# Where float64 weights are converted and where the softmax is divided: one change to a fused attention and Fourier-mixing kernel

## The chip, the cores and the metric

The kernel runs on 1 core of one Trainium2 chip. The metric is the device time in microseconds (us) of one launch; the median of seven runs is given. The engines of the core are TensorE (PE in the profile, its weight loads PEld), VectorE (DVE), ScalarE (ACT), GpSimd (POOL) and SyncE (SP), which here issues nearly all transfers. TensorE writes to PSUM; the other engines take its results from there.

## The reference

Eight batches of eight heads, 576 rows, head size 64. Attention keeps only the scores within `tau` of the row's maximum. Its result, with the heads joined to 512 columns, is transformed by a Fourier transform over rows and columns (the real part is kept), added to itself, normalized and sent through two matrix products with a ReLU between.

```python
scores = (1 / sqrt(64)) * q @ k.T                       # per batch and head
thresh = max(scores, axis=-1) - tau
scores = where(scores >= thresh, scores, -1e9)
attn = exp(scores - max(scores)); attn /= sum(attn) + 1e-9
x = (attn @ v) joined to (8, 576, 512)
mixed = real(fft(fft(x, axis=1), axis=2))
u = x + mixed
un = (u - mean(u)) / sqrt(var(u) + 1e-6)
out = u + maximum(un @ w_ch1, 0) @ w_ch2                # w_ch1 (512, 2048), w_ch2 (2048, 512)
```

`w_ch1` and `w_ch2` come as float64. [...]

## The kernel before

**Pairs and steps.** Two heads make a pair, four pairs a batch, so there are 32 pairs. A pair has five steps: four of 128 rows of q and one of the last 64. That makes 160 steps, 20 in each batch; step `i` belongs to pair `i // 5`. A step runs

- `scores` (L410): PE multiplies q and k into two PSUM tiles `sc`, of which there are two, so the next scores wait until DVE has read the last ones;
- `softmax` (L437): DVE finds the maxima (L448), ACT takes the exponential (L456) and the threshold (L460), DVE cuts off and sums (L464), adds 1e-9 and takes the reciprocal `den` (L476);
- `transposed_weights` (L493) of the step before: PE transposes `e` into `pe` (L516) and `pw` (L533), ACT copies them out to `ends` (L523, L528) and `e_t` (L535, L537);
- for the last step of a pair `weighted_values` (L542): PE multiplies with `v` into `pv` (L554), and the result goes to `x`. For half of the pairs two rows of `x` are then swapped by four small transfers.

`prep_pair` (L379) transposes q and k of the next pair (`pq`, `pk`, `pt`), and DVE and ACT copy them to `qT` and `kT`.

**Where the softmax is divided.** In the first two batches POOL spreads `den` over a tile `rec` (L486), PE transposes `rec` too (L519) beside `e` into `pe`, both parts go to `ends`, and DVE multiplies `pv` with it (L562). From the third batch on (`normalized`, L405) DVE multiplies `e` by `den` at once (L480), there is no `rec`, and ACT copies `pv` to `x` (L560).

**Mixing and channels.** When a batch's `x` is there, it is folded (`fold_rows`, `fold_halves`: POOL, for the last pair DVE) and goes through `mixing` (L624: PE `py`, `pa`; the sums into `u_t` by DVE and POOL). Then `channels` (L717) takes groups of 384 rows: `ph` with `w1` (L744), ReLU into the four sections `h0` to `h3` (L750 on ACT, L752 on DVE), then `po` with `w2` (L765) and the result out. Both are generators, which `fill` (L789) advances three times in each step from the second batch on, by a budget of PE work, so that PE's order mixes attention and channels. PSUM holds four tiles `mm` for all of this. In the first batch `busy` (L102) puts products of a constant (L109, `pd`) into the order as filler, two units in steps before `NCHUNK` and one after, each unit two matmul records.

**Conversion.** A chunk is 512 KB of float64. `convert` (L273) is a generator of five parts: the transfer (L280); two bit operations on DVE (L290, L293); three activations on ACT (L298, L301, L304); one product and sum on DVE (L306); two products on POOL (L311, L312). `w1` has 16 chunks, `w2` has 16. A chunk needs room for its raw bits and for the powers. In the first batch the room is a section of `h` (`staged`), and steps 0 to 19 convert `w1` and the last four chunks of `w2` (`first_chunk`, `NCHUNK` = 20), one started in each step. In the second batch `PLAN` (L887) lists the other 12: the step, the chunk, its room (a pair of chunks of `w2` not yet written, a section of `h`, or the tile `tmp`) and the step that issues its transfer. The powers then go to the part of `u_t` that the second batch does not use yet. `advance` runs the next part of a step's chunk. In the second batch the order is by hand on all engines (`second_batch`, L930); from the third on it is by hand on PE alone, and a scheduler places the others.

```python
w2_chunk(j):  pairs_w2 holds chunks (0,1), (2,3), (4,5); chunks 6 to 15 have tiles of their own
room 0, 1, 2: the raw bits lie in pairs_w2[room], that is, in both chunks of that pair
```

Of the kernel before, what the change touches and what calls it, by code (L numbers as in the profile page):

```python
# [47 lines left out]
def kernel(  # L48
# [270 lines left out]
    def staged(n, src, dst):  # L319
        stage = sb.tile([128, 3, WC], INT32, tag=f"h{n % 4}", bufs=1, name="stage")  # L320
        return chunk(src, dst, stage[:, 0:2, :], stage[:, 2, :])

    def first_chunk(n):

        if n >= HID // WC * ND:
            return staged(n, *w2_chunk(NJ - 1 - (n - HID // WC * ND)))
        g, c = divmod(n, ND)
        cols = slice(WC * g, WC * (g + 1))
        return staged(n, w_ch1[128 * c : 128 * (c + 1), cols], w1[c][:, cols])
# [4 lines left out]
    def second_chunk(j, room):  # L334


        if room == "h":
            return staged(3, *w2_chunk(j))
        if room == "tmp":
            raw = sb.tile([128, 2 * WC], INT32, tag="tmp", bufs=1, name="stage")[:, :]  # L340
        else:
            raw = pairs_w2[room][:, :].bitcast(INT32)
        power = u_t[:, j % ND, S : S + WC].bitcast(INT32)
        return chunk(*w2_chunk(j), raw.rearrange("p (c n) -> p c n", c=2), power)
# [34 lines left out]
    def prep_pair(n):  # L379
# [22 lines left out]
        if n + 1 < B * NPAIR:  # L402
            load_pair(n + 1)

    def normalized(n):  # L405


        return n >= 2 * NPAIR

# [27 lines left out]
    def softmax(i, between=None, meanwhile=None):  # L437
# [38 lines left out]
        nc.vector.reciprocal(den[:, 0:nh], den[:, 0:nh])  # L476
        rec = None
        if normalized(i // NT):
            for j in range(nh):
                nc.vector.tensor_scalar(  # L480
                    out=e[:, S * j : S * (j + 1)], in0=e[:, S * j : S * (j + 1)],
                    scalar1=den[:, j : j + 1], scalar2=None, op0=ALU.mult,
                )
        else:
            rec = sb.tile([128, 2 * D], FP32, tag="rec", name="rec")
            nc.gpsimd.tensor_copy(  # L486
                rec[:, :].rearrange("p (j d) -> p j d", j=nh), _repeated(den[:, 0:nh], 2 * D // nh)
            )
        if t == 4:
# [3 lines left out]
    def transposed_weights(i):  # L493
# [22 lines left out]
        nc.tensor.transpose(pe[:, 0, :], e[:, 512:640], ident[:, :])  # L516
        parts = 1
        if rec is not None:
            nc.tensor.transpose(pe[:, 1, :], rec[:, :], ident[:, :])  # L519
            parts = 2  # L520
        if t < 4:
            qs = slice(128 * t, 128 * t + 128)
            nc.scalar.copy(ends[:, 0:parts, qs], pe[:, 0:parts, :])  # L523
        else:
            qs = slice(512, S)
            for j in range(2):
                hp = slice(64 * j, 64 * j + 64)
                nc.scalar.copy(ends[hp, 0:parts, qs], pe[hp, 0:parts, hp])  # L528
        for j in range(2 if t < 4 else 1):
# [12 lines left out]
    def weighted_values(n):  # L542
# [6 lines left out]
        for h in range(2):  # L549
            cols = slice(HALF * h, HALF * (h + 1))  # L550
            pv = ps.tile([128, 512], FP32, tag="mm", bufs=4, name="pv")
            for c in range(5):
                for j in range(2):
# [4 lines left out]
                    )  # L558
            if normalized(n):
                nc.scalar.copy(x[:, cols], pv[:, 0:HALF])  # L560
            else:
                nc.vector.tensor_tensor(  # L562
                    out=x[:, cols], in0=pv[:, 0:HALF], in1=ends[:, 1, cols], op=ALU.mult
                )
        if p % 2:
# [151 lines left out]
    def channels(g):  # L717
# [4 lines left out]
        rstd = sb.tile([128, nt], FP32, tag="rstd", name="rstd")  # L722
        hT = [sb.tile([128, 4, GT], FP32, tag=f"h{i}", bufs=1, name=f"h{i}") for i in range(4)]

# [15 lines left out]

        for j in range(NJ):
            ph = ps.tile([128, 512], FP32, tag="mm", bufs=4, name="ph")
            for c in range(ND):
# [61 lines left out]
    def step(i):  # L805
# [28 lines left out]
        if i > 0 and i + 3 < NCHUNK:  # L834
            chunks[i + 3] = first_chunk(i + 3)
        if t == 2 and n > 0:
# [6 lines left out]
    after = []  # L843
    NCHUNK = HID // WC * ND + 4

# [19 lines left out]

    chunks = {0: first_chunk(0)}
    raw = load_dim()
    load_seq()
    chunks[1] = first_chunk(1)
    prep_pair(0)  # L870
    load_v(0)
    chunks[2] = first_chunk(2)
    chunks[3] = first_chunk(3)
    load_v(1)
# [9 lines left out]
    while after:  # L884
        after.pop(0)[1]()

    PLAN = (  # L887
        (2, 11, 0, 0), (3, 10, 1, 0), (4, 9, 2, 0), (5, 8, 0, 3), (6, 7, 1, 4), (7, 6, 2, 5),
        (8, 5, 0, 6), (9, 4, 1, 7), (10, 3, "h", 7), (11, 2, 0, 9), (12, 1, "tmp", 9),
        (14, 0, "tmp", 13),  # L890
    )
    chunks = {-1: chunks.pop(NCHUNK - 1)}

    def advance(at):
        if at in chunks:
            next(chunks[at], None)

    def transfers(first):
        for at, j, room, issue in PLAN:
            if issue == first:  # L900
                chunks[at] = second_chunk(j, room)

# [27 lines left out]
    def second_batch(i):  # L930
# [6 lines left out]
        softmax(i, None, lambda: advance(first - 1))  # L937
        if first - 1 in chunks:
            next(chunks.pop(first - 1), None)
        transfers(first)  # L940
# [13 lines left out]
        elif first == 1:  # L954
            mix(3)
            transposed_weights(i - 1)
            busy(2)
            mix(2)
        elif first == 2:
            mix(2)  # L960
# [9 lines left out]
        else:  # L970
            fill()
            transposed_weights(i - 1)
            advance(first)
            advance(first)
            if t == 3:
                prep_pair(n + 1)
            fill()
            fill()
# [85 lines left out]
```

## Time and profile before

| what | us |
|---|---|
| median of 7 runs | 1754.01 (1752.21 to 1757.78) |
| time of the profiled execution | 1754.01 |
| its span, first to last instruction | 1752.0 |
| first batch (reciprocal of step 0 to that of step 20) | 15.4 to 142.8 |
| second batch (to the reciprocal of step 40) | 142.8 to 302.7 |
| last attention step's reciprocal (step 159) | 1526.6 |

Some groups of the page, with the mean time of one and the count:

| line, engine | what | mean ns | count |
|---|---|---|---|
| L744 PE | `ph`, 384 columns | 490 | 1536 |
| L765 PE | `po`, 512 columns | 597 | 1152 |
| L533 PE | transposes of `e` | 274 | 1152 |
| L519 PE | transposes of `rec` | 277 | 40 |
| L480 DVE | `e` times `den` | 572 | 216 |
| L486 POOL | `rec` | 369 | 40 |
| L560 ACT | `pv` to `x` | 399 | 48 |
| L562 DVE | `pv` times `rec` to `x` | 450 | 16 |

Matmuls are pipelined: the mean is the duration of one, and the distance between two starts is shorter. The granted clock over the whole span is 0.997. The page's chain of waits lies on PE for 82% of the span, on DVE for 7% and on ACT for 4%.

### The profile page before, as it was taken

What the parts mean: (1) busy time and instruction counts of PE and PEld (TensorE: products, weight loads), DVE (VectorE), ACT (ScalarE), POOL (GpSimd) and SP (SyncE); (2) the same over time, 40 slices, a digit from 0 to 9 for tenths busy, and PEclk for the clock granted to TensorE, in tenths of its full rate; (3) what the DMA queues carried; (4) which work ended last, traced back from release to release, by engine and by line L of the source; (5) the groups of instructions that cost most, each with busy time, mean ns of one, the idle gap of its engine ahead of it and who ended that gap; (6) DMA issues with size and microseconds to landing.
All of it is one profiled execution on the core that took longest, in us unless ns stands there. A gap on an engine that the chain in (4) does not pass through costs nothing.

```text
span 1752.0 us, 21426 instructions
## 1 busy us (share of the span) xinstructions
PE 1708.3 (98%) x7772; PEld 978.9 (56%) x7772; DVE 858.4 (49%) x2123; ACT 662.4 (38%) x1510; POOL 317.3 (18%) x499
## 2 busy tenths in 40 slices
PE   8988989999999999999999999999999999999999
PEld 4555655555565566566555556556556556555453
DVE  6786765544445555544433655644334555511010
ACT  5674664323243444334233435333224334411010
POOL 5575542030110311020110212011101031010000
PEclk9999999999999999999999999999999999999999
DMA  5331311100100101010010110100001010000000
GB/s 158 107 100 57 101 55 36 33 14 14 32 21 20 27 22 33 21 33 14 17 30 14 27 33 22 27 26 24 10 26 27 24 29 9 1 12 7 12 7 18
DMA packets 130350, 57.00 MB, mean 33 GB/s; under 512 B 121123, under 2 KB 121125, under 8 KB 130246
## 3 DMA queue, kind: packets, MB, share of 16 engines
q1 hardware_dynamic: 128854, 55.35, 11.8%
q8 instruction: 62, 1.02, 0.2%
q10 hardware_dynamic: 1392, 0.30, 0.1%
q14 instruction: 42, 0.34, 0.1%
HBM read 46.02 MB, written 9.44 MB: 32 GB/s over the span
## 4 chain that ended last, share of the span: by engine, by line
PE 82%; DVE 7%; ACT 4%; issue 3%; POOL 1%; DMA 1%; SPq 1%; ACTq 0%; DVEq 0%; POOLq 0%
PE ph L744 27%; PE po L765 27%; PE pv L554 8%; PE sc L420 7%; PE pw L533 5%; DVE e L464 2%; PE sc L431 2%; ACT e L456 1%; PE py L653 1%; DVE neg L448 1%; PE pa L670 1%; PE pa L674 1%; PE pe L516 1%; PE pn L728 1%; PE pk L394 1%
## 5 line engine op out<-in xcount | busy, mean ns | idle before, releaser
L744 PE MATMUL ph<-u_t,w 128*128 128x384 f32 x1536 | 522.9, 490 | 4.0 <-ACT ends L523 1.2
L765 PE MATMUL po<-w,h 128*128 128x512 f32 x1152 | 524.3, 597 | 0.0
L744 PEld LDWEIGHTS ph<-u_t,w 128*128 128x128 f32 x1536 | 282.7, 190 | 191.7 <-issue 13.9
L448 DVE TENSOR_REDUCE neg<-sc 128x1 f32<-128x576 f32 x288 | 205.7, 751 | 357.3 <-PE sc L420 281.0
L456 ACT ACTIVATE e<-sc,neg 128x576 f32<-128x576 f32 x288 | 211.9, 736 | 352.8 <-DVE neg L448 351.8
L765 PEld LDWEIGHTS po<-w,h 128*128 128x128 f32 x1152 | 207.9, 190 | 221.4 <-issue 220.2
L464 DVE SCALAR_TENSOR_TENSOR e<-sc,thr,e 128x576 f32<-128x576 f32 x288 | 227.4, 814 | 86.2 <-ACT thr L460 82.9
L420 PE MATMUL sc<-kT,qT 64*128 64x288 f32 x1024 | 166.8, 431 | 4.5 <-DVE e L464 3.8
L533 PE MATMUL pw<-ident,e 128*128 128x128 f32 x1152 | 155.0, 274 | 11.9 <-ACT kT L395 5.8
L533 PEld LDWEIGHTS pw<-ident,e 128*128 128x128 f32 x1152 | 130.9, 141 | 39.5 <-issue 14.4
L750 ACT ACTIVATE h<-ph 128x384 f32<-128x384 f32 x96 | 47.1, 491 | 263.5 <-PE ph L744 263.4
L535 ACT COPY e_t<-pw 128x512 f32<-128x512 f32 x256 | 140.0, 593 | 11.0 <-PE pw L533 10.3
L420 PEld LDWEIGHTS sc<-kT,qT 64*128 64x128 f32 x1024 | 92.9, 187 | 83.6 <-issue 58.0
L585 POOL TENSOR_TENSOR half<-x 128x287 f32<-128x287 f32 x48 | 40.3, 860 | 542.2 <-ACT x L560 238.8
L692 POOL TENSOR_TENSOR u_t<-x,tmp 128x289 f32<-128x289 f32 (+1 forms) x47 | 36.3, 782 | 539.7 <-DVE tmp L689 539.3
L752 DVE TENSOR_SCALAR h<-ph 128x384 f32<-128x384 f32 x96 | 53.1, 554 | 162.0 <-PE ph L744 161.9
L480 DVE TENSOR_SCALAR e<-e,den 128x576 f32<-128x576 f32 x216 | 115.4, 572 | 3.4
L772 DVE SCALAR_TENSOR_TENSOR u<-po,rstd,u 128x512 f32<-128x512 f32 x36 | 26.9, 747 | 123.1 <-PE po L765 123.1
L560 ACT COPY x<-pv 128x288 f32<-128x288 f32 x48 | 19.2, 399 | 149.9 <-PE pv L554 133.8
L554 PE MATMUL pv<-e_t,v_rev 128*64 128x288 f32 x512 | 68.3, 409 | 0.6 <-ACT h L750 0.6
L554 PE MATMUL pv<-e_t,v_in 128*64 128x288 f32 x512 | 68.4, 409 | 0.0
L523 ACT COPY ends<-pe 128x128 f32<-128x128 f32 (+1 forms) x128 | 37.2, 291 | 71.7 <-PE pe L516 62.9
(147 smaller groups left out, 1499.8 us busy)
## 6 DMA issues: line engine op xcount, KB each, us to landing
stage<-in_moe_w_ch_dram SPq DMA_DIRECT2D x23, 512.0 KB, 4.0
out_dram<-u SPq DMA_DIRECT2D x36, 256.0 KB, 2.0
qk_in<-in_q_dram SPq DMA_DIRECT2D x64, 128.0 KB, 2.4
v_in<-in_v_dram SPq DMA_DIRECT2D x64, 128.0 KB, 2.3
w<-in_moe_w_ch_dram SPq DMA_DIRECT2D x9, 512.0 KB, 3.7
qk_in<-in_k_dram SPq DMA_DIRECT2D x31, 128.0 KB, 2.4
qk_in<-in_k_dram SPq DMA_DIRECT2D x31, 64.0 KB, 2.3
qk_in<-in_k_dram SPq DMA_DIRECT2D x93, 16.0 KB, 2.1
```

Source lines behind the costliest of these rows:

```text
L420: nc.tensor.matmul(sc[j][:, c, 0:HALF], qT[hp, 128 * t : 128 * t + 128], kT[hp, HALF * c : HALF * (c + 1)], start=True, stop=True,)
L448: nc.vector.tensor_reduce(out=neg[:, j : j + 1], in_=sc[j][:, :, 0:HALF], axis=AXIS_XY, op=ALU.max, negate=True,)
L456: nc.scalar.activation(out=ej, in_=sc[j][:, :, 0:HALF], func=ACT.Exp, bias=neg[:, j : j + 1], scale=1.0)
L464: nc.vector.scalar_tensor_tensor(out=ej, in0=sc[j][:, :, 0:HALF], scalar=thr[:, j : j + 1], in1=ej, op0=ALU.is_ge, op1=ALU.mult, accum_out ...
L480: nc.vector.tensor_scalar(out=e[:, S * j : S * (j + 1)], in0=e[:, S * j : S * (j + 1)], scalar1=den[:, j : j + 1], scalar2=None, op0=ALU.mult,
L533: nc.tensor.transpose(pw[:, c, :], e[:, c0 : c0 + 128], ident[:, :])
L535: nc.scalar.copy(e_t[:, 4 * j : 4 * j + 4, qs], pw[:, :, :])
L554: nc.tensor.matmul(pv[64 * j : 64 * j + 64, 0:HALF], vt[:, 2 * c + j, :], e_t[:, 4 * j + c, cols] if c < 4 else ends[:, 0, cols], start=(c ...
L744: nc.tensor.matmul(ph[:, 0:GT], w1[c][:, 128 * j : 128 * (j + 1)], u_t[:, c, c0 : c0 + GT], start=(c == 0), stop=(c == ND - 1),)
L750: nc.scalar.activation(out=ht, in_=ph[:, 0:GT], func=ACT.Relu)
L752: nc.vector.tensor_relu(ht, ph[:, 0:GT])
L765: nc.tensor.matmul(po[:, :], hT[j // 4][:, j % 4, 128 * t : 128 * (t + 1)], w2[j], start=(j == 0), stop=(j == NJ - 1),)
```

## The change

It has four parts.

1. `normalized` goes. In all 160 steps POOL makes `rec`, PE transposes it, `ends` gets two parts, and DVE multiplies `pv` with it.
2. The first batch converts only `w1` (16 chunks, `w1_chunk`). As `NCHUNK` falls to 16, steps 16 to 19 have one unit of filler where they had two (three units in all, since step 16 has none).
3. `PLAN` has all 16 chunks of `w2`. The first four lie in `h0` to `h3`; steps 5, 8 and 9 convert two chunks each; a step holds a list of chunks, and step 1 advances too. `channels` allocates a section of `h` when it comes to it and not all four at once.
4. In the second batch `prep_pair` comes after the second `fill` of its step and not before. In PE's order this moves q and k in step 38 alone: two `po` products come ahead of `pq`.

```diff
-        rec = None
-        if normalized(i // NT):
-            for j in range(nh):
-                nc.vector.tensor_scalar(
-                    out=e[:, S * j : S * (j + 1)], in0=e[:, S * j : S * (j + 1)],
-                    scalar1=den[:, j : j + 1], scalar2=None, op0=ALU.mult,
-                )
-        else:
-            rec = sb.tile([128, 2 * D], FP32, tag="rec", name="rec")
-            nc.gpsimd.tensor_copy(
-                rec[:, :].rearrange("p (j d) -> p j d", j=nh), _repeated(den[:, 0:nh], 2 * D // nh)
-            )
+        rec = sb.tile([128, 2 * D], FP32, tag="rec", name="rec")
+        nc.gpsimd.tensor_copy(
+            rec[:, :].rearrange("p (j d) -> p j d", j=nh), _repeated(den[:, 0:nh], 2 * D // nh)
+        )
...
-        parts = 1
-        if rec is not None:
-            nc.tensor.transpose(pe[:, 1, :], rec[:, :], ident[:, :])
-            parts = 2
+        nc.tensor.transpose(pe[:, 1, :], rec[:, :], ident[:, :])
...
-            if normalized(n):
-                nc.scalar.copy(x[:, cols], pv[:, 0:HALF])
-            else:
-                nc.vector.tensor_tensor(
-                    out=x[:, cols], in0=pv[:, 0:HALF], in1=ends[:, 1, cols], op=ALU.mult
-                )
+            nc.vector.tensor_tensor(
+                out=x[:, cols], in0=pv[:, 0:HALF], in1=ends[:, 1, cols], op=ALU.mult
+            )
...
-        hT = [sb.tile([128, 4, GT], FP32, tag=f"h{i}", bufs=1, name=f"h{i}") for i in range(4)]
+        hT = []
...
         for j in range(NJ):
+            if j % 4 == 0:
+                i = j // 4
+                hT.append(sb.tile([128, 4, GT], FP32, tag=f"h{i}", bufs=1, name=f"h{i}"))
...
-    NCHUNK = HID // WC * ND + 4
+    NCHUNK = HID // WC * ND
...
     PLAN = (
-        (2, 11, 0, 0), (3, 10, 1, 0), (4, 9, 2, 0), (5, 8, 0, 3), (6, 7, 1, 4), (7, 6, 2, 5),
-        (8, 5, 0, 6), (9, 4, 1, 7), (10, 3, "h", 7), (11, 2, 0, 9), (12, 1, "tmp", 9),
-        (14, 0, "tmp", 13),
+        (1, 15, "h0", 0), (2, 14, "h1", 0), (3, 13, "h2", 0), (4, 12, "h3", 0),
+        (5, 11, "0", 0), (5, 10, "1", 0), (6, 9, "2", 0), (7, 8, "h3", 5),
+        (8, 7, "0", 6), (8, 6, "1", 6), (9, 5, "tmp", 4), (9, 4, "h3", 8),
+        (10, 3, "0", 9), (11, 2, "h3", 10), (12, 0, "tmp", 10), (14, 1, "tmp", 13),
     )
-    chunks = {-1: chunks.pop(NCHUNK - 1)}
+    chunks = {}
...
     def advance(at):
-        if at in chunks:
-            next(chunks[at], None)
+        for run in chunks.get(at, ()):
+            next(run, None)
...
         elif first == 1:
             mix(3)
             transposed_weights(i - 1)
             busy(2)
             mix(2)
+            advance(first)
+            advance(first)
...
             advance(first)
             advance(first)
+            fill()
             if t == 3:
                 prep_pair(n + 1)
             fill()
-            fill()
```

## The prediction

> **What bounds the kernel now.** I read the page's busy shares first, then a table of windows by stage, then the timeline where the stages meet.
>
> ```profile
> PE 1708.3 (98%) x7772; PEld 978.9 (56%) x7772; DVE 858.4 (49%) x2123; ACT 662.4 (38%) x1510; POOL 317.3 (18%) x499
> ```
>
> PE is busy for 98% of the span, but that average hides stages. In the windows below the columns are: length, then the busy time of PE, PEld, DVE, ACT and POOL, the granted clock, the DMA share and GB/s. 115:143 is the end of the first batch, 142:310 the second batch, the other four the third to eighth batch (steps 40 to 159).
>
> ```profile
> 115.00:143.00 28.00, 22.91 (x135) 13.52 (x133) 25.07 (x60) 21.02 (x43) 20.99 (x24) 1.00 0.35 100
> 142.00:310.00 168.00, 156.34 (x844) 94.61 (x841) 110.04 (x268) 90.07 (x197) 68.34 (x90) 0.99 0.21 59
> ...
> 310.00:541.90 231.90, 230.11 (x997) 131.28 (x996) 104.93 (x260) 79.87 (x185) 25.05 (x42) 1.00 0.09 22
> 541.90:953.50 411.60, 409.08 (x1905) 236.12 (x1904) 205.42 (x517) 153.04 (x357) 49.03 (x84) 1.00 0.10 24
> 953.50:1365.00 411.50, 408.98 (x1905) 236.12 (x1904) 206.26 (x517) 153.13 (x357) 49.19 (x84) 1.00 0.10 24
> 1365.00:1530.00 165.00, 162.85 (x824) 95.84 (x823) 94.49 (x242) 69.52 (x163) 23.86 (x40) 1.00 0.07 17
> ```
>
> From 310 to 1530 PE lacks only 1220.0 - 1211.0 = 9.0 us, while DVE is busy for half of the time: there an instruction more on PE lengthens the run, and one less on DVE does nothing. From 115 to 143 it is the other way round: DVE 25.1 of 28 us, and PE's 22.9 contain filler (L109). In the second batch PE lacks 11.7 us, so only what makes PE wait counts.
>
> **Third to eighth batch: 120 transposes come back.** In each of the 120 steps from step 40 on, `rec` is transposed on PE once more, as L519 does in the first 40 steps. Its price is the distance between starts, not its duration:
>
> ```profile
> 122.27 0.27 PE L516 MATMUL pe<-ident,e 128*128 128x128 f32 x1
> ...
> 122.37 0.27 PE L519 MATMUL pe<-ident,rec 128*128 128x128 f32 x1
> ...
> 122.48 1.04 PE L533 MATMUL pw<-ident,e 128*128 128x128 f32 x8
> ...
> 542.15 0.27 PE L516 MATMUL pe<-ident,e 128*128 128x128 f32 x1
> ...
> 542.26 0.60 PE L533 MATMUL pw<-ident,e 128*128 128x128 f32 x4
> ```
>
> The columns are start and duration in us. With `rec` the first `pw` starts 0.21 us after `pe`, without it 0.11; the eight of one group take 1.04, so (1.04 - 0.27) / 7 = 0.11 each. 120 x 0.109 = **+13.1 us**. Lower bound: PE's idle 9.0 us all hide it, 4.1. Upper bound: none overlaps its neighbours, 120 x 0.272 = 32.6. I take 13.1, as the trace shows that very sequence at that distance in the first 40 steps and the groups of eight at it everywhere.
>
> The Trainium skill ("TensorE: Matmul & The Clock Gate", Part 4: PE-mode transpose) gives about 275 ns for a transpose in a kernel's context; priced so, the 120 would be 33 us and the whole forecast near 1781.6. That figure agrees with the duration of one in this trace (272), but the distance of starts decides, so the measurement is followed.
>
> Beside it, at no cost:
> - 216 multiplications of `e` leave DVE (L480, 115.4 us). Nothing waits on DVE there; the gain is between 0 and the 9.0 us, and PE's few idle places in that stretch are mostly released by ACT (`ends`, `kT`) or POOL: 0.
> - 120 copies of `rec` come to POOL (L486, median 316 ns, 38 us) beside 147 of 1220 us busy. The transpose waits for the copy, and all of PE's order stands behind it, but it comes one step later (8 to 10 us), so the copy has a step's time. In the 40 existing ones PE and PEld waited 3.3 us in all; at that rate 120 would cost 10 us. Most of those stood behind conversions on POOL, which the later batches lack: 0, upper end 10.
> - The product of L562 (450 ns x48 on DVE) replaces ACT's copy L560 (399 ns x48). `ends` is held until it ends; the next writer of `ends` comes after scores (1.24) and a unit of `ph` (2.85), over 4 us of cover. Without the cover 48 x 0.45 = 21.6.
> - `ends` is copied 256 wide instead of 128 (0.37 against 0.28 us): 96 x 0.09 = 8.6 us of ACT, hidden by four PSUM buffers.
>
> **End of the first batch: four conversions leave.** Chunks 16 to 19 were w2's. Each costs DVE 0.487 + 0.596 + 0.778 = 1.86, ACT 2.0 and POOL 2.6 us. What it costs the chain is how long a finished score waits for its reduction behind them:
>
> ```profile
> 128.94 1.20 PE L431 MATMUL sc<-kT,qT 64*64 64x288 f32 x10 [0.17 <-DVE e L464]
> ...
> 130.12 0.79 DVE L290 TENSOR_SCALAR w<-stage 128x512 int32<-128x512 int32 x1
> ...
> 130.82 1.01 DVE L293 TENSOR_SCALAR stage<-stage 128x512 int32<-128x512 int32 x1
> ...
> 131.75 1.28 DVE L306 SCALAR_TENSOR_TENSOR w<-stage,w 128x512 f32<-128x512 uint32 x1
> ...
> 132.96 0.74 DVE L448 TENSOR_REDUCE neg<-sc 128x1 f32<-128x576 f32 x1
> ```
>
> Here the scores end at 130.14, the reduction starts at 132.96: 2.8 us. In the two steps before the same gap is 0.4 (120.51 to 120.89) and 0.45 (125.77 to 126.22), in the step after it nothing. Sum **-3.7 us**; ends 0 and -7.4 (all four conversions' DVE time). The second batch starts that much earlier, and PE's chain follows.
>
> Three filler pairs (L109, 0.86 us per unit of two matmuls) go in steps 17 to 19; they run while PE waits, so 0. If the granted clock fell for it, the price is what the one dip shows at 255.83: eight `ph` in 3.79 instead of 2.85, 0.9 us. The skill speaks against taking filler away (same page, "Why this matters for your kernels": no idle gaps over about 3 us); at the rate of the dip it would add 0.9 us. PE's longest gap in that window is 2.83 us, and the clock read 1.00.
>
> **Second batch: sixteen conversions for twelve.** Where they delay PE:
> - Chunk 15 is new in steps 21 and 22. Its DVE pair (1.08) comes after 161.77, its three ACT operations (2.0) before the exponential that started at 162.47: that then starts near 164.3, and `sin` (L685, 164.38), for which PE's `pw` waits already, 1.8 later. **+1.8**; ends 0 and 3.1.
> - Two chunks in steps 25, 28, 29. The second adds DVE 0.498 + 0.821, ACT 2.0, in the next step DVE 0.8. Step 25 has the 4.8 us of `pv` as cover; in step 26 the second L306 stands before the product that frees the scores (PE came at 201.71, it ended at 201.59): +0.8. In step 28 it fills a DVE wait of 2.24 us on POOL: 0. In step 29 ACT's 2.0 stand before the exponential (225.74) and the ReLU (227.17) for which `pv` waited: +1.7. **+2.5**; ends 0 and 10 (three times 1.3 + 2.0).
> - Other rooms for the chunks take waits away, and q and k go one unit later in step 38:
>
> ```profile
> 250.32 0.69 DVE L290 TENSOR_SCALAR w<-stage 128x512 int32<-128x512 int32 x1 [3.04 <-POOL w L312]
> ...
> 252.16 0.66 PE L389 MATMUL pq<-ident,qk_in 128*128 128x128 f32 x4 [2.56 <-DVE h L752]
> ...
> 254.71 1.12 PE L394 MATMUL pk<-ident,qk_in 128*128 128x128 f32 x4 [1.90 <-ACT ends L523]
> ...
> 288.93 0.66 PE L389 MATMUL pq<-ident,qk_in 128*128 128x128 f32 x4 [1.48 <-ACT ends L523]
> ```
>
> Brackets hold the idle time before and its releaser. Chunk 1 overwrites half of the tile in which chunk 2 is still staged, so DVE waits for POOL, a ReLU is late, PE stands for 2.56 + 1.90, and the dip adds 0.9: 5.4. A like wait of 3.06 at 231.87 ends in a PE gap of 1.2 at 239.02. In the new order chunks 4 and 5, 2 and 3, 0 and 1 come a step or more after the last reader of their pair. With the 1.5 at 288.93 (two `po` products, 1.7 us, now run there) 8.1 us can go. But three transfers (chunks 4, 3, 2) now have one step between the POOL product that frees their room and their use: 2.9 to 5.6 us of POOL and 4.0 to land, against steps of 6.5 to 11.6, so some wait comes back. **-6.0**; ends -8.1 and 0.
> - SP: seven transfers of 512 KB instead of three stand before `load_v` in the first step. At the page's 158 GB/s they take 23 us; that `v` is used five steps (45 us) on: 0. In step 30 the swap of `x` rows stands behind a transfer that waits for POOL, about when the swap was issued before (236.4): 0.
> - Sections of `h` allocated as reached: an order of buffers only, 0; the last chunk in `h3` ends two steps before its section.
>
> **Sum** against the profiled execution (1754.01 us, span 1752.0 and 2.0 around it; its time is the median of the seven): 13.1 - 3.7 + 1.8 + 2.5 - 6.0 = **+7.7, 1761.7 us**. The last 222 us (`ph` and `po` alone) are untouched.
>
> **Rivals.**
> - *Faster.* The first two batches give back more than the transposes take. At hand are PE's idle 5.1 and 11.7 us and 2.6 of filler, 19.4; to be faster by 3.5 it takes 16.6, 86% of it: 1750.5 at that point. For it: DVE is the bound at 115 to 143. Against: of the 11.7 only 7.1 stand at the four gaps named above; the rest, at the folds, the mixing and the first `ph`, keeps what makes it. Chance 0.06.
> - *Nothing measurable.* As forecast, but waits and conversions at their good ends, half of chunk 15 and the pairs hidden: 13.1 - 5.5 + 1 + 1 - 8.1 = +1.5, 1755.5. Chance 0.14.
> - *Late `rec`.* POOL takes its order strictly; where a fold of `x` (about 4 us, waiting for the swap's DMA) stands before the copy, PE's transpose waits. At 1 us in each of 12 pairs with a swap +12: 1773.7. Against: in the built order the copy stands before those folds. Chance 0.08.
> - *Crowded second batch.* The doubled steps cost 10 instead of 2.5 and the waits come back: 13.1 - 3.7 + 1.8 + 10 = +21, 1775. Chance 0.08.
>
> The forecast itself keeps 0.64, with its own range of 1757.5 to 1767.
>
> **Range.** 1755 to 1769 leaves out the faster case, a part of the second and most of the last two. What a measurement can tell from no change is 0.2%, 3.5 us: faster 0.06, same 0.14, slower 0.80.
>
> **What would show it.** From the third batch on each pair of batches 411.5 + 40 x 0.109 = 415.9 long, with 160 `rec` transposes in all and PE's idle no larger; step 20's reciprocal near 139 instead of 142.8; the gap before `pq` at 252 gone. It is wrong if PE shows waits on POOL's `rec` after 310, or if the second batch ends more than 8 us earlier or any later than before.

## The result and the profile after

The changed kernel takes 1759.46 us (median, 1758.03 to 1760.61); the kernel before, measured beside it, 1753.78. The ratio is 1.0028, with a 95% interval of 1.0021 to 1.0035: slower by about 4.9 us (the medians are 5.7 apart). Between the two profiled executions the span grows by 6.0 us, from 1752.0 to 1758.0; the trace below explains these 6.0.

First the busy shares and the windows of the changed kernel, in the columns and the stretches used before:

```profile
PE 1716.3 (98%) x7886; PEld 989.9 (56%) x7886; DVE 776.6 (44%) x1955; ACT 658.3 (37%) x1462; POOL 348.4 (20%) x619
```

```profile
115.00:143.00 28.00, 25.84 (x165) 15.76 (x162) 20.16 (x58) 14.21 (x31) 11.63 (x18) 1.00 0.33 102
142.00:310.00 168.00, 155.69 (x826) 94.39 (x825) 124.95 (x282) 99.47 (x213) 78.09 (x96) 0.99 0.23 67
...
541.90:953.50 411.60, 409.31 (x1934) 238.26 (x1933) 174.69 (x454) 150.34 (x338) 59.26 (x123) 1.00 0.10 24
```

PE has 8.0 us more to do in all, DVE 81.8 less. In the end of the first batch DVE falls from 25.1 to 20.2 us of 28; in the second batch it rises from 110.0 to 125.0 of 168; from 541.9 to 953.5, in the fourth and fifth, PE is as full as it was.

Where the time goes shows best when one marks the end of DVE's reciprocal in each step and subtracts the kernel before. The first 16 steps run the same work in both, so in this table each kernel is set to 0 at step 16 (us, minus is earlier):

| kernel | 20 | 23 | 26 | 29 | 30 | 32 | 34 | 40 | 159 |
|---|---|---|---|---|---|---|---|---|---|
| the change | -4.4 | -2.2 | -0.1 | -0.3 | +2.9 | +2.6 | -1.9 | -3.7 | +6.2 |
| e1_rec_all | 0.0 | 0.0 | 0.0 | 0.0 | 0.0 | 0.0 | 0.0 | 0.0 | +9.8 |
| e2_w2_only | -4.4 | -2.2 | -0.1 | -0.3 | +2.9 | +2.7 | -1.9 | -3.6 | -3.7 |
| e5_no_double_in_29 | -4.4 | -2.2 | -0.1 | -0.3 | +0.4 | +3.0 | +1.8 | +1.3 | +1.4 |
| e9_one_double | -4.4 | -2.2 | -2.2 | -1.1 | -0.4 | -0.4 | +4.1 | +7.6 | +7.6 |
| e10_double_in_30 | -4.4 | -2.2 | -0.1 | -0.3 | +2.2 | +2.8 | -1.3 | -3.0 | -3.0 |
| e12_loaded_early | -4.4 | -2.2 | -0.1 | -0.3 | +0.4 | +1.4 | -0.9 | -2.6 | -2.7 |

So the first batch gives 4.4 us; the second gives back 0.7 of them on balance, with 2.2 lost at steps 21 to 23, 2.1 at step 26, 3.2 at step 30, and 4.8 won by step 34 and 1.7 at step 39; and the third to eighth batch lose 9.9.

The end of the first batch, in the timeline of the changed kernel (start, duration):

```profile
127.15 1.20 PE L423 MATMUL sc<-kT,qT 64*64 64x288 f32 x10 [0.27 <-DVE e L456]
...
128.38 0.76 DVE L440 TENSOR_REDUCE neg<-sc 128x1 f32<-128x576 f32 x1
```

The scores end at 128.35 and the reduction starts 0.03 later. Before, 2.8 us of conversion stood between the two.

The returned transposes, in the same timeline:

```profile
553.71 0.27 PE L500 MATMUL pe<-ident,e 128*128 128x128 f32 x1
553.82 0.27 PE L501 MATMUL pe<-ident,rec 128*128 128x128 f32 x1
553.92 1.04 PE L514 MATMUL pw<-ident,e 128*128 128x128 f32 x8
```

`pw` starts 0.21 us after `pe`, as in the first forty steps before. And the stalls at the two places where q and k are transposed late in the second batch:

```profile
251.63 0.60 PE L386 MATMUL pq<-ident,qk_in 128*128 128x128 f32 x4
253.53 0.66 PE L391 MATMUL pk<-ident,qk_in 128*128 128x128 f32 x4 [1.30 <-ACT ends L504]
...
286.73 0.60 PE L386 MATMUL pq<-ident,qk_in 128*128 128x128 f32 x4
```

Of 2.56, 1.90 and 1.48 us only 1.30 is left. A new stall is in step 29, in the same view:

```profile
222.06 0.42 DVE L290 TENSOR_SCALAR w<-stage 128x512 int32<-128x512 int32 x1
222.07 1.54 POOL L311 TENSOR_TENSOR w<-w,u_t 128x512 f32<-128x512 f32 x1
222.39 1.50 DVE L293 TENSOR_SCALAR u_t<-stage 128x512 int32<-128x512 int32 x1
223.68 1.37 POOL L312 TENSOR_TENSOR w<-w,w 128x512 f32<-128x512 f32 x1
223.81 1.52 DVE L290 TENSOR_SCALAR w<-stage 128x512 int32<-128x512 int32 x1
...
225.25 1.51 DVE L293 TENSOR_SCALAR stage<-stage 128x512 int32<-128x512 int32 x1
...
226.68 1.41 DVE L440 TENSOR_REDUCE neg<-sc 128x1 f32<-128x576 f32 x2
...
227.98 0.72 ACT L448 ACTIVATE e<-sc,neg 128x576 f32<-128x576 f32 x1
...
229.94 3.85 PE L535 MATMUL pv<-e_t,v_rev 128*64 128x288 f32 x16 [3.42 <-ACT h L731]
```

The kernel before, at the same place:

```profile
223.02 1.50 DVE L293 TENSOR_SCALAR u_t<-w 128x512 int32<-128x512 int32 x1
...
224.44 1.41 DVE L448 TENSOR_REDUCE neg<-sc 128x1 f32<-128x576 f32 x2
...
225.74 0.72 ACT L456 ACTIVATE e<-sc,neg 128x576 f32<-128x576 f32 x1
...
227.71 2.16 PE L554 MATMUL pv<-e_t,v_rev 128*64 128x288 f32 x16 [0.56 <-ACT h L750]
```

The four bit operations take 4.7 us in all. The first takes 0.42; the other three start while a product runs on POOL, take 1.5 each and end about 0.3 us after it. The kernel before has one such operation there (L293, 1.50), not three. The scores of the step were there at 222.65; their reduction starts at 226.68, the exponential and a ReLU follow on ACT, and PE stands 3.42 us before `pv`, where it stood 0.56. From the start of the reduction to that of the exponential it is 1.30 us in both kernels, so what came late is the reduction, on DVE. Then sixteen `pv` take 3.85 us instead of 2.16; the granted clock is 0.5 from 230.2 to 233.6, that is, for most of them.

A page of the Trainium skill bears on these rows ("SBUF — State Buffer", section "SBUF: two separate sides"): it describes the port pair that DVE and GpSimd share as an exclusive lock, held for a whole instruction, on which the loser waits. It says so for DVE operations in a two-port mode or with two inputs in SBUF; in which mode these ran, no run here shows. The ends of L293 (223.89) and of the second L290 (225.33) behind those of L311 (223.61) and L312 (225.05) agree with it.

### The profile page after: what moved, and what is told of

Read it like the earlier page. It is cut to its first block, busy times and chain, and to the rows that moved or that the text cites. A ratio compares the mean times of both kernels' runs of the same rounds, so it can differ in the third digit from the quotient of the medians.

```text
span 1758.0 us, 21685 instructions
## 1 busy us (share of the span) xinstructions
PE 1716.3 (98%) x7886; PEld 989.9 (56%) x7886; DVE 776.6 (44%) x1955; ACT 658.3 (37%) x1462; POOL 348.4 (20%) x619
## 4 chain that ended last, share of the span: by engine, by line
PE 84%; DVE 8%; ACT 4%; DMA 1%; SPq 1%; issue 1%; POOL 1%; ACTq 0%; DVEq 0%; POOLq 0%
PE ph L725 27%; PE po L746 27%; PE pv L535 8%; PE sc L412 7%; PE pw L514 5%; DVE e L456 2%; PE sc L423 2%; ACT e L448 1%; DVE neg L440 1%; PE py L631 1%; PE pa L648 1%; PE pa L652 1%; PE pn L706 1%; PE pe L500 1%; PE pe L501 1%
## 5 line engine op out<-in xcount | busy, mean ns | idle before, releaser
L470 POOL COPY rec<-den 128x128 f32<-128x128 f32 x160 | 50.5, 316 | 1024.8 <-DVE den L468 710.0
L540 DVE TENSOR_TENSOR x<-pv,ends 128x288 f32<-128x288 f32 x64 | 29.0, 456 | 174.0 <-PE pv L535 174.0
L504 ACT COPY ends<-pe 128x256 f32<-128x256 f32 x128 | 47.7, 372 | 85.1 <-PE pe L501 78.1
L535 PEld LDWEIGHTS pv<-e_t,v_rev 128*64 128x64 f32 x512 | 35.9, 139 | 35.6 <-issue 7.4
L535 PEld LDWEIGHTS pv<-e_t,v_in 128*64 128x64 f32 x512 | 35.8, 138 | 33.0 <-issue 6.4
```

What stands on the lines that cost most here:

```text
L470: nc.gpsimd.tensor_copy(rec[:, :].rearrange("p (j d) -> p j d", j=nh), _repeated(den[:, 0:nh], 2 * D // nh))
L504: nc.scalar.copy(ends[:, :, qs], pe[:, 0:2, :])
L535: nc.tensor.matmul(pv[64 * j : 64 * j + 64, 0:HALF], vt[:, 2 * c + j, :], e_t[:, 4 * j + c, cols] if c < 4 else ends[:, 0, cols], start=(c ...
```

## The experiments

Each is a change to one of the two kernels or to an earlier run, as the text says; line numbers differ by a few from kernel to kernel. Ratios are against the kernel before, run beside it.

**The two parts apart.** First part one alone, in the kernel before:

```diff
-        return n >= 2 * NPAIR
+        return n >= B * NPAIR
```

> The kernel before with part one of the change alone: rec is copied, transposed and multiplied into x in all 160 steps, the w2 conversions stay where they were. Theory A (from the two traces: PE gains 10.8 us of work and loses 0.9 us of idle time in batches three to eight): 1754 + 9.9 = about 1763.7, PE's idle time there about 8, steps 40 to 159 longer by 9.5 to 10.5 us, the stretch before step 40 within 0.5 us of before. Theory B (nothing else is relieved, each transpose costs its distance of starts of 0.109 us): +13.1, 1767. Rival C (late rec on POOL): above 1770, with PE waits on rec.

Measured: 1762.95 us, ratio 1.0048 [1.0032, 1.0064]. The first 40 steps are unchanged, and between the reciprocals of steps 40 and 159 the run takes 1233.72 us instead of 1223.87: +9.85, as in the changed kernel (1233.77). PE is busy for 10.8 us more and idle for 8.0 instead of 9.0. Theory A; late `rec` is out, since PE has no wait on it there.

Then the rest alone: the changed kernel with `normalized`, L480, `parts` and L560 put back as they were before.

```diff
+    def normalized(n):
+        return n >= 2 * NPAIR
```

> The changed kernel with part one undone: from the third batch on the weights are divided on DVE and rec is not transposed, as before; all of w2 is converted in the second batch by the changed plan, q and k one unit later. Theory A (the two parts add up; the reciprocal of step 40 came 4.0 us earlier in the changed kernel): about 1749.8, a ratio of 0.9977. Theory B (the gain at the end of the first batch is only borrowed, and part one is what kept it): 1754, no difference. Theory C (the removed waits are worth the 6.0 us I took, and it is part one that was dearer): 1748 or less.

Measured: 1749.75 us, 0.9966 [0.9952, 0.9979]. Steps 16 to 40 run as in the changed kernel to 0.1 us, and nothing changes after. Theory A: the parts add up, and the lead of 3.6 us is not borrowed. This kernel beats both.

**The price of a transpose and of a multiplication.** In the kernel before, from the third batch on:

```diff
         if rec is not None:
             nc.tensor.transpose(pe[:, 1, :], rec[:, :], ident[:, :])
             parts = 2
+        else:
+            nc.tensor.transpose(pe[:, 1, :], e[:, 512:640], ident[:, :])
```

> The kernel before, in which from the third batch on a second transpose of the same 128 columns of e follows the first one on PE (120 more, its result is not used); DVE, ACT and POOL have the work they had. This prices the transpose by itself. If the distance of starts of 0.109 us is the price and the relief of the changed kernel comes from DVE's multiplications: +13.1, 1767. If a part of the transposes lies in PE's idle time anyway: +9.9 or less, 1764. If the duration is the price: +32.6, 1786.

```diff
         if normalized(i // NT):
-            for j in range(nh):
-                nc.vector.tensor_scalar(
...
+            pass
```

> The kernel before without the 216 multiplications of e on DVE from the third batch on: the weights of those batches are left undivided, which leaves out the division there. This prices DVE's relief by itself. If DVE's multiplications keep PE waiting: -3.0 (13.1 less 9.9), about 1751. If nothing on the path that sets the end waits for them, as I predicted: within 0.5 of 1754, and the 3 us come from the transposes' side.

Measured: 1766.68 us, 1.0057 [1.0044, 1.0071], and 1751.41 us, 0.9978 [0.9969, 0.9987]. Between steps 40 and 159 the second transpose costs 11.1 us, between two of the values expected (9.9 and 13.1), and the missing multiplications gain 3.6. (From step 16 to step 40 both kernels also lose some 3 us, though they are the kernel before to the instruction there; see the clock below.) At its place the transpose costs what I had said, by the timeline of the kernel with the second transpose:

```profile
559.57 0.27 PE L516 MATMUL pe<-ident,e 128*128 128x128 f32 x1
559.68 0.27 PE L522 MATMUL pe<-ident,e 128*128 128x128 f32 x1
559.79 1.04 PE L535 MATMUL pw<-ident,e 128*128 128x128 f32 x8
```

0.22 us from `pe` to `pw`, 120 x 0.109 = 13.1, of which 2.0 vanish: PE's idle falls from 9.0 to 7.6 us, and its busy time grows by 12.5 us, 0.104 per transpose, and not by 13.1. And DVE's multiplications did cost something. PE's waits from 302 to 1540 us (sum, times, longest) in the kernel before and in the one without them:

```profile
PE py L653 <- ACT ends L523: 2.3, 3, 0.8
PE py L653 <- ACT kT L395: 2.1, 4, 0.5
```

```profile
PE pw L529 <- ACT y_e L659: 1.5, 3, 0.5
PE py L649 <- DVE qT L390: 1.2, 4, 0.3
```

No wait ever named the multiplication. The first two waits, 4.4 us, are gone, and the last two, 2.7, are new; PE's idle from step 40 to 159 falls from 9.0 to 6.3 us. That ACT's copies come later when DVE's chain does is my reading of it. The two results don't add: 11.1 less 3.6 is 7.5, and e1_rec_all, with both changes, measured 9.85, so all that lies beside its transposes is worth 1.25. Both may draw on the same idle time of PE; but e1_rec_all also has what these two runs lack, POOL's copies of `rec`, the wider `ends` and DVE's product in place of ACT's copy, and no run sets these apart.

**The double in step 29.** From here on the base is the second kernel, e2_w2_only (1749.75). Chunk 4 leaves step 29 and the last chunks come a step later:

```diff
-        (9, 5, "tmp", 4), (9, 4, "h3", 8), (10, 3, "0", 9), (11, 2, "h3", 10),
-        (12, 0, "tmp", 10), (14, 1, "tmp", 13),
+        (9, 5, "tmp", 4), (10, 4, "1", 9), (11, 3, "0", 9), (12, 2, "h3", 9),
+        (13, 1, "tmp", 10), (15, 0, "tmp", 14),
```

> The second batch of the changed kernel with the division on DVE from the third batch on (that pair of parts gave 1749.8), and a plan without a double step 29: chunk 4 goes to step 30, chunk 3 to 31, 2 to 32, 1 to 33, 0 to 35. Steps 25 and 28 keep two chunks. Theory A (the second chunk of step 29 stretches DVE's conversions beside POOL and makes the eight pv run at half clock; the reciprocal of step 30 came 3.1 us later for it): about 3 less, 1746.7, with step 30's reciprocal near 228.7 and no pv group of 3.8. Theory B (what is gained there is lost again at the steps that now hold a chunk, 33 and 35): 1749.8, no difference.

Measured: 1754.90 us, 1.0003 [0.9994, 1.0012]. At step 30 the table shows +0.4 instead of +2.9, so the double does cost its 2.5 there. But the gain is lost again, at other steps than theory B named, as this kernel's timeline shows:

```profile
238.30 2.85 PE L744 MATMUL ph<-u_t,w 128*128 128x384 f32 x8 [1.74 <-ACT ends L520]
...
242.70 1.00 DVE L290 TENSOR_SCALAR w<-w 128x512 int32<-128x512 int32 x1 [2.60 <-POOL w L312]
...
246.35 4.54 PE L744 MATMUL ph<-u_t,w 128*128 128x384 f32 x8 [2.79 <-ACT h L750]
```

The 2.60 us on DVE are my plan's fault: chunk 4 lay in the pair of chunks 2 and 3, and chunk 3, a step later, writes into that pair. It is the wait that the change had removed from the kernel before (there chunks 2 and 1), built anew. Later PE waits 2.1 us for the first `po`, since chunk 0 is ready only in step 36.

> The changed kernel with the division on DVE from the third batch on (1749.8) and the second chunk of step 29 moved to step 30, and no chunk staged in a pair that the next one or two write: 5 in a quarter of h in step 29, 4 in the pair of chunks 0 and 1 and 3 in tmp in step 30, then 2, 0 and 1 in steps 31, 32 and 34 as in the changed kernel. Theory A (the double in step 29 costs about 3 with its dip; without a late reader of the room, the loss of the run without a double 29 doesn't come back, and DVE has 4 us of idle time in the stretch after step 30): about 3 less, 1746.7, no stall over 1 us before the pv near 230 and none on ACT between 236 and 250. Theory B (the double costs the same wherever it stands): 1749.8. Theory C (the waits near 238 and 246 came from the later steps and not from the room of chunk 4): 1753 or more.

```diff
-        (8, 7, "0", 6), (8, 6, "1", 6), (9, 5, "tmp", 4), (9, 4, "h3", 8),
-        (10, 3, "0", 9), (11, 2, "h3", 10), (12, 0, "tmp", 10), (14, 1, "tmp", 13),
+        (8, 7, "0", 6), (8, 6, "1", 6), (9, 5, "h3", 8), (10, 4, "0", 9),
+        (10, 3, "tmp", 4), (11, 2, "h3", 10), (12, 0, "tmp", 11), (14, 1, "tmp", 13),
```

Measured: 1749.69 us, 0.9971 [0.9958, 0.9983]: no better than the base. The stall of 2.79 near 246 is gone, and with it DVE's wait of 2.60, so the room of chunk 4 was the cause of most of it (in the next run, where PE comes earlier, 0.63 stand at that place); but the stall before `pv` stays, with one chunk in the step; its timeline, with SP's issue of the transfer first:

```profile
219.41 0.33 SPq L280 DMA_DIRECT2D stage<-in_moe_w_ch_dram  x1
...
223.33 1.01 DVE L290 TENSOR_SCALAR w<-stage 128x512 int32<-128x512 int32 x1 [1.83 <-DMA stage<-in_moe_w_ch_dram]
...
225.69 1.41 DVE L445 TENSOR_REDUCE neg<-sc 128x1 f32<-128x576 f32 x2
...
228.94 3.34 PE L551 MATMUL pv<-e_t,v_rev 128*64 128x288 f32 x16 [3.06 <-ACT h L750]
```

The room's transfer goes out when POOL frees it, one step before its use, and DVE, whose order is fixed, waits 1.83 us for it with the reduction behind. Load it earlier, in the kernel of e10_double_in_30:

```diff
-        (7, 8, "h3", 5),
+        (7, 8, "h2", 4),
...
-        (9, 5, "h3", 8),
+        (9, 5, "h3", 5),
```

> As the run with the double in step 30, but chunk 8 is staged in the third quarter of h and chunk 5 in the fourth, whose transfer is then issued in step 25 instead of 28 (there its data landed at 223.3, DVE had waited 1.83 us for it, and the score's reduction stood behind the conversion until 225.7 while the scores had ended at 222.0). Theory A (that late transfer, not the second chunk, kept the stall of 3.1 us before pv): the stall falls to the 0.56 of the run without a double 29, the lead at step 30 is 1.8 larger, and the time about 1.8 less: 1747.9 (span 1746.2). Theory B (the chunk of step 29 costs this in any room): 1749.7, the stall stays near 3.

Measured: 1750.13 us, 0.9974 [0.9964, 0.9985]. The stall is the expected one, and step 30 comes 1.8 us earlier against the table's line of e10. Yet the time stays, and this kernel's timeline shows why:

```profile
227.39 2.16 PE L551 MATMUL pv<-e_t,v_rev 128*64 128x288 f32 x16 [0.57 <-ACT h L750]
...
239.50 2.85 PE L744 MATMUL ph<-u_t,w 128*128 128x384 f32 x8 [1.85 <-ACT ends L520]
...
245.39 2.85 PE L744 MATMUL ph<-u_t,w 128*128 128x384 f32 x8 [0.63 <-ACT h L750]
...
253.14 0.66 PE L391 MATMUL pk<-ident,qk_in 128*128 128x128 f32 x4 [1.76 <-ACT ends L520]
...
254.11 4.54 PE L744 MATMUL ph<-u_t,w 128*128 128x384 f32 x8 [0.15 <-ACT e_t L532]
```

The stall before `pv` gave up 2.5 us (3.06 to 0.57). PE waits 1.85 and 0.63 us, 2.5 together, at 239.50 and 245.39, where e10_double_in_30 has no wait: at the first place ACT copies `ends` behind two exponentials, and these wait for DVE's reduction, which starts 3.2 us after its scores ended (233.63 to 236.79), behind the conversions of the doubled step 30 on DVE and ACT; in e10_double_in_30, where PE comes later, that gap is 0.3. Besides, the dip of the clock that sat behind the stall at 229 now sits behind the one at 253: eight `ph` take 4.54 us instead of 2.85, 1.7 lost. In e10_double_in_30 the dip cost as much (sixteen `pv` 3.34 instead of 2.16, four more 1.18 instead of 0.66), so its move alone gains or loses nothing. In windows of 3 us, the granted clock in the third column from the end:

```profile
255.00:258.00 3.00, 3.00 (x14) 1.55 (x14) 1.54 (x8) 2.07 (x4) 2.75 (x6) 1.00 0.00 0
230.00:233.00 3.00, 3.00 (x14) 1.57 (x16) 2.00 (x9) 2.17 (x6) 1.53 (x2) 0.54 0.03 5
```

```profile
255.00:258.00 3.00, 3.00 (x6) 1.57 (x5) 1.21 (x5) 1.14 (x2) 2.75 (x4) 0.51 0.03 5
230.00:233.00 3.00, 3.00 (x28) 1.67 (x26) 3.00 (x3) 2.07 (x4) 2.38 (x2) 1.00 0.01 3
```

The first two lines are the changed kernel (0.54 at 230, 1.00 at 255), the others this one (1.00 and 0.51).

**Chunk 15 and the double in step 25.** Two plans, of which the diffs show the lines that matter here: the first begins a step later, the second begins as before and has one chunk in step 25. Neither has a double in step 29. Both stage chunk 2 over chunk 1 once that is converted, so that they leave chunk 1 out of `w2`, and DVE waits for that transfer (6.85 us at 258 in the second); what follows step 33 says nothing.

```diff
-        (1, 15, "h0", 0), (2, 14, "h1", 0), (3, 13, "h2", 0), (4, 12, "h3", 0),
+        (2, 15, "h0", 0), (3, 14, "h1", 0), (4, 13, "h2", 0), (5, 12, "h3", 0),
...
```

> As the kernel without a double step 29, and no chunk in step 21 either: chunk 15 begins in step 22, 14 in 23, 13 in 24, 12 joins 11 in 25, then 10 and 9 alone, 8 and 7 together in 28, and 6 to 0 in steps 29 to 35. Theory A (chunk 15 in steps 21 and 22 costs the 2.3 us by which step 23's reciprocal lost its lead): about 2.3 less than without that edit, 1744.5, the reciprocal of step 23 near 174.4. Theory B (the exponential of step 22 has to wait for some chunk's ACT work in any order, now chunk 15's in step 22): 0.

Measured: 1763.75 us, 1.0049 [1.0037, 1.0062]. At step 23 the lead is 4.5 us instead of 2.2, so chunk 15 did cost 2.3 there. At step 24, 7.5 us are lost: chunk 15 then holds the first section of `h` until POOL's product ends at 178.2, ACT waits 4.8 us to write the first ReLU into it, and PE 5.75.

```diff
-        (5, 11, "0", 0), (5, 10, "1", 0), (6, 9, "2", 0), (7, 8, "h3", 5),
+        (5, 11, "0", 0), (6, 10, "1", 0), (7, 9, "2", 0), (8, 8, "h3", 5),
...
```

> As the kernel without a double step 29, and step 25 has one chunk too: 15 to 9 one each in steps 21 to 27, 8 and 7 together in 28, 6 to 0 in steps 29 to 35. Theory A (the second chunk of step 25 costs the 2.1 us by which step 26's reciprocal lost its lead): about 2 less than with that double, 1744.7, the reciprocal of step 26 near 200.2. Theory B (it is the fuller steps after it that set the time): 0 or more.

Measured: 1760.12 us, 1.0026 [1.0016, 1.0037]. At step 26 the lead is 2.2 us instead of 0.1: the second chunk of step 25 costs 2.1. Theory A holds as far as that; the end of the run can't tell. At step 33 this plan leads the kernel before by 3.3 us, where the changed one leads by 0.3.

> As the run with the double in step 30, but the conversions begin in step 20, whose stretch has 13 us of idle POOL, 8.9 of ACT and 3.8 of DVE: 15 in step 20, 14 to 8 one each in steps 21 to 27, 7 and 6 in 28, then as there; chunks 15 and 14 are loaded before step 20. Theory A (chunk 15's 2.3 us in steps 21 and 22 and the 2.1 us of the double in step 25 go as well): 4.4 less than with the double in step 30, about 1742.3. Theory B (a chunk in step 20 delays the mixing, which has its copies on ACT there, by what it saves later): no less, or more; step 21's reciprocal is then more than 1 us late against its place in the changed kernel.

```diff
+        (0, 15, "h0", -1), (1, 14, "h1", -1), (2, 13, "h2", 0), (3, 12, "h3", 0),
+        (4, 11, "0", 0), (5, 10, "1", 0), (6, 9, "2", 0), (7, 8, "h2", 3),
+        (8, 7, "0", 5), (8, 6, "1", 6), (9, 5, "h3", 4), (10, 4, "0", 9),
...
             mix(3)
+            advance(first)
+            advance(first)
...
+    transfers(-1)
```

Measured: 1751.33 us, 0.9981 [0.9972, 0.9990]: theory B. By step 22 it stands at +3.3 where the base has -2.7. Of these 6.0 us 2.3 were lost by step 20, before any conversion of the second batch, under the dip of the clock at 117.7; the other 3.7 in steps 20 to 22. Chunk 15's three activations run from 150.06 to 151.85 between the copies of the mixing, and PE waits 2.3 us for `y_o` at 153.84; a second dip, at 155.2, lies in the same stretch. 8.9 us of idle ACT were no room, since they stood before the copies and not among them.

**q and k one unit later, alone,** in the kernel before:

```diff
+            fill()
             if t == 3:
                 prep_pair(n + 1)
             fill()
-            fill()
```

> The kernel before with one edit: in the second batch q and k of a pair are transposed one unit of filling later. Theory A (the wait of 1.48 before pq at 288.93 goes, the other two pairs stand as they did or gain a little): -1.7, 1752.3; the reciprocal of step 39 1.7 earlier, all before step 33 unchanged. Theory B (the unit that takes its place waits for the same thing, and the gain seen in the changed kernel in step 39 came from the plan): 0.

Measured: 1753.38 us, 0.9990 [0.9979, 1.0001]. From step 38 to 39 it gains the 1.7 us, and nothing at step 33: theory A by its place; the total is too near to one to tell.

**Division on POOL.** In the base, L480's multiplications on GpSimd:

```diff
-                nc.vector.tensor_scalar(
+                nc.gpsimd.tensor_scalar(
```

> The changed kernel with the weights divided from the third batch on, as before the change (1749.8), but the 216 multiplications of e stand on POOL instead of DVE. Theory A (what the run without the multiplications gained, 3.6 us between the reciprocals of steps 40 and 159, is had by any engine but DVE that is done a step later; POOL has 1070 of 1220 us idle there): about 3, 1746.8. Theory B (POOL's product beside DVE stretches DVE's work, as beside the conversions in step 29, or POOL takes so long that the transposes of the next step wait): 1750 or more, with PE waiting on e from POOL or DVE's operations longer than in the kernel before.

Measured: 1778.59 us, 1.0133 [1.0114, 1.0153]. Theory B, by its second half: DVE's reductions and cut-offs keep their 752 and 815 ns, but PE waits. The group in the kernel before and here (busy, mean ns), and the longest waits of PE:

```profile
L480 DVE TENSOR_SCALAR e<-e,den 128x576 f32<-128x576 f32 x72 | 37.8, 562 | 1.2
```

```profile
L477 POOL TENSOR_SCALAR e<-e,den 128x576 f32<-128x576 f32 x72 | 124.3, 1736 | 218.5 <-DVE den L473 176.2 <-PE pe L513 16.5 <-PE pw L530 13.4
```

```profile
PE pe L513 <- POOL e L477: 12.9, 10, 2.5
PE ph L744 <- POOL u_t L689: 8.9, 3, 4.1
```

1.74 us instead of 0.56, and POOL does its work in order: `e` stands behind folds, and the mixing's sums behind `e`.

## Why the prediction was right, step by step

The forecast of +7.7 stands against +6.0 in the trace and +4.9 by the ratio; the signs of its terms and most of their places held. That the sum came so near is in part luck: the transposes were 3.2 us too dear and the doubled steps 2.6 too cheap, which nearly cancels. The measured column goes by the steps at which time is lost or won, and that is not always the place of the cause.

| term | said | measured |
|---|---|---|
| transposes from the third batch on, with all that lies beside them | +13.1 | +9.9 |
| end of the first batch | -3.7 | -4.4 |
| chunk 15 | +1.8 | +2.2 |
| doubled steps 25, 28, 29 | +2.5 | +5.1 (2.1, -0.2, 3.2) |
| waits removed | -6.0 | -6.5 (4.8 by step 34, 1.7 at step 39) |
| first 16 steps, same work | 0 | -0.3 |
| sum | +7.7 | +6.0 |

- *Transposes.* The distance of starts is the price at the place, the duration of 0.272 us is not: 11.1 us for 120 alone, 93 ns each. The 275 ns of the Trainium skill ("TensorE: Matmul & The Clock Gate", Part 4), which would have made 33 us, is the duration here too (272 ns). What failed is the size of what lies beside: idle time hides 1.4 us of the transposes, where 9.0 was kept as a bound and 0 taken; and "Nothing waits on DVE there" is wrong, as the multiplications alone are worth 3.6 us (e4_undivided). With all that the change puts beside the transposes 1.25 of it is left. PE at 98% was not PE without slack.
- *End of the first batch.* Right, with its cause: where 2.8 us of conversion stood before a reduction, 0.03 are left. The filler taken away shows no cost: the half-clock window at 110.8 of the changed kernel is not in e2_w2_only, which has the same filler, and one at 109.6 is in e1_rec_all, which has all the filler of before.
- *Doubled steps.* The term that was mis-sized, and in step 29 also put on the wrong engine. A second chunk was priced by its operations' durations alone (0.498 + 0.821 on DVE); started beside POOL's products of the chunk before they take 1.5 each. In step 25 the 0.8 for the second product is 0.6, but the stretched pair makes ACT's activations and copies late, DVE's next work waits for those copies, and the reduction starts 1.5 us after its scores instead of 0.03: 2.1 together. In step 29 the 1.7 was for three ACT operations before the exponential. They held it up by nothing new, as it starts 1.30 us after its reduction begins in both kernels; the reduction is 2.9 us late behind the second pair on DVE, and the second product adds 0.3: 3.2. The dip at 230 lies behind that, at `pv`, and is not in the 3.2.
- *Waits removed.* Right in sum, and e5_no_double_in_29 showed the mechanism by bringing one back. But the 4.8 by step 34 holds two dips, which I did not take apart: the one at 230, which makes `pv` 1.7 us longer in the changed kernel, and the one at 254.5 of the kernel before, which is not there any more. The reservation that "three transfers now have one step" was right too: e10_double_in_30 shows such a transfer costing 1.83 us on DVE, in a stall of 3.06 on PE.
- *Rivals.* Late `rec`: none after step 40. Crowded second batch: half of the way there, 5.1 of 10. The faster case was far: it needed 16.6 us given back, and 10.9 were.
- *Signs named.* Reciprocal of step 20: "near 139", 138.2. `rec` transposes: 160. The gap before `pq` at 252: gone. 40 steps in the fourth and fifth batch: 415.9 said, 414.9 measured (540.2 to 955.1). PE's idle from step 40 to 159: no larger, 8.0 after 9.0.

## What to carry to other kernels

Where one engine is busy for 98%, price an added instruction by the distance of starts at its place, and expect the run to pay less: here 11.1 of 13.1 us for the transposes alone and 9.9 with all that came beside them. When preparing work is packed into a hand-written order, ask of each staging room who writes next to it and when it was freed: a tile that a later item overwrites, and a transfer issued one step before its use, each made DVE, which does its work in order, wait 1.8 to 2.6 us before its next result. When a second piece of such work goes into a step, ask what runs on the other engines beside it: its bit operations took 1.5 us there, where the step's first took 0.42. A stall taken out is not always a gain: look whether the engine waits the same time a few steps on, as PE did for 1.85 and 0.63 us after 2.5 had gone.

## What had not been expected of the hardware

Every profiled execution has windows in which the granted clock is 0.5, each 3.4 us long or two or three times that (but for one at the very end), and they do not sit at fixed instructions: with the same work the stall of 2.8 us near 135 has none behind it in the kernel before and in e1_rec_all, and one of 6.8 us in e3_second_transpose, e4_undivided and e6_pair_later. From step 16 to step 34 these three lose 2.9 to 3.3 us against the kernel before, though they do the same work there. The executions of one kernel differ too: e12_loaded_early took 1747.75 us in the one with a mean granted clock of 1.000 and 1751.87 in the one with 0.995. So the places of the dips in a trace are those of one execution.

I listed all stretches over 2.6 us in the fourteen profiles in which PE runs nothing but transposes or stands still. A window of half clock begins within them or at most 1.6 us behind them in 5 of 127 stretches below 3.4 us, 7 of 49 from 3.4 to 4.5, 12 of 21 from 4.5 to 6 and 13 of 13 above 6. So transposes do not seem to hold the clock up, as far as such a count can tell: at 248 to 256 us of the kernel before the two stalls are 2.6 and 1.9 us, but with the transposes around them 7.5 us pass without a product. The Trainium skill ("TensorE: Matmul & The Clock Gate", Part 4: PE-mode transpose) says that a transpose is not counted as busy in the way a product is, which agrees; its rule of no idle gap over some 3 us (section "Why this matters for your kernels") would then count the stretch, not the gap. Eleven windows, at 18, 24, 110, 229, 287 and 294 us of some runs, follow no such stretch, and no run here set the transposes apart from the stalls, so the cause is argued and not shown.
